# Attention and mixture of experts in one kernel: the transposes of K and pooled Q in half tiles, two groups a pair

## The chip, the cores and the metric

The kernel runs on one core of a Trainium2 chip. The metric is device time in microseconds (us) of one execution. Everything is float32 but a few small routing tables.

The engines are named as in the profile: PE (TensorE matmul; PEld is its weight load), DVE (VectorE), ACT (ScalarE), POOL (GpSimd) and SP (SyncE, which issues most DMA transfers). PE and the others meet in PSUM, the accumulator memory of eight banks; a bank holds 512 float32 in each of 128 partitions.

## The reference

q, k and v are 8 batches of 8 heads of 1152 rows of 64. Neighbouring rows of q are averaged, so 576 queries attend to 1152 keys. The 4608 attention rows of 512 then go through a mixture of 8 experts, each row through the one with the largest logit.

```python
q_pool = q.reshape(B, H, S // 2, 2, D).mean(axis=3)
scores = np.matmul(q_pool, k.transpose(0, 1, 3, 2)) / np.sqrt(D)
attn = np.exp(scores - scores.max(-1, keepdims=True))
x = heads_side_by_side(np.matmul(attn / (attn.sum(-1, keepdims=True) + 1e-9), v))
e, gate = argmax_and_its_probability(x @ w_gate)
out[row] = gate[row] * (np.maximum(x[row] @ w1[e[row]], 0) @ w2[e[row]])
```

## The kernel before

**Work.** Attention goes by batch (8) and by pair of heads (4 a batch, 32 in all). For a pair, `load_pair` loads K (`kn`), Q (`qn`) and V (`vn`), adds neighbouring rows of Q on POOL (`qp`; the first pair on DVE), orders K by row on ACT (`kp`), and turns both on PE, so that the 2 x 64 features of the two heads lie on the 128 partitions: `kT` (128 x 1152) and `qT` (128 x 576). PE turns a tile by a matmul with an identity (`nc.tensor.transpose`); the result lies in PSUM, and ACT copies it to `kT` or `qT`. This is done in groups, by the function `piece`.

`scores` then works a pair in two halves of 288 queries. For each of 9 chunks of 128 keys PE multiplies in four tiles of 64 x 64 at once into a buffer `st` of two banks, and DVE takes it out to `s` and finds a minimum on the way (line 525). There are two `st` buffers. After nine chunks PE spreads the minimum over the partitions (`spread`, line 543, which uses an `st` buffer too), DVE makes the bias, and ACT takes the exponent in three steps of three chunks (line 553). POOL adds the nine chunks to one in three steps, the folds (line 599), and PE adds up what they leave (line 608, into the bank `sums`). PE multiplies the exponents with V in nine chunks (`values`, line 624), again in four tiles.

There are two `fold` buffers and four buffers `s`. In the last three pairs PE does the sums without folds (line 594).

At the end of a batch the routing runs: row sums (line 644), logits (698), a turn (705), then on DVE the best expert, on PE the ranks (739 to 744), on DVE the places, and six scatters by POOL to lists in memory (`lists`, line 799). All of it uses the bank `sums`, which the next batch's first sum of folds needs. After the last batches POOL gathers the rows of the experts (`xr`, line 899), and the mixture of experts follows with two matmul stages (lines 1113 and 1141).

**Order.** A planner written in the kernel (`Flow`) sets the order on each engine. Each step has an engine, an assumed time and a key (a due time), and holds buffers. The planner plays the steps through and emits them in the order in which they came up, the lowest key first; a step whose buffer is not free is passed by. A step on PE has a tile shape (`COLS`, `QUADS`, or none for whole tiles); the planner stays with a shape as long as another with nearly the same key is ready. On the chip the engines run their lists in this order and wait for each other by semaphores.

PSUM before: two `st` buffers of two banks, one bank `m` (function `bank`) that holds a group of transposes, `pa` of two banks for the values, and `sums`.

## Time and profile before

| | |
|---|---|
| three timed runs, median (lowest to highest) | 1312.04 us (1309.75 to 1315.79) |
| the profiled execution, its own time | 1304.89 us |
| its span in the trace | 1303.3 us |
| busy over the span: PE, DVE, ACT, POOL | 94%, 59%, 49%, 66% |
| attention | until about 785 us, the mixture of experts behind it |

The span runs from the first to the last instruction of the trace. Busy time of PE counts a matmul until its modelled end, so matmuls side by side overlap in it. In the slices of the page each digit is a fortieth of the span, in tenths.

### The profile page before, as it was taken

What the parts mean: (1) busy time and instruction counts of PE and PEld (TensorE: products, weight loads), DVE (VectorE), ACT (ScalarE), POOL (GpSimd) and SP (SyncE); (2) the same over time, 40 slices, a digit from 0 to 9 for tenths busy, and PEclk for the clock granted to TensorE, in tenths of its full rate; (3) what the DMA queues carried; (4) which work ended last, traced back from release to release, by engine and by line L of the source; (5) the groups of instructions that cost most, each with busy time, mean ns of one, the idle gap of its engine ahead of it and who ended that gap; (6) DMA issues with size and microseconds to landing.
All of it is one profiled execution on the core that took longest, in us unless ns stands there. A gap on an engine that the chain in (4) does not pass through costs nothing. (4 is left out here: it accounts for less than half of the span.)

```text
span 1303.3 us, 32720 instructions
## 1 busy us (share of the span) xinstructions
PE 1222.0 (94%) x13677; PEld 844.5 (65%) x13677; DVE 771.5 (59%) x2080; ACT 637.5 (49%) x832; POOL 862.1 (66%) x539
## 2 busy tenths in 40 slices
PE   7999999999999999999999598898689889999995
PEld 3555555555555555555555157797578779899895
DVE  5777777767767768768776067663334435425440
ACT  4666666656666666666574046332223323424440
POOL 2999799798998998998992701577475755300110
PEclk8999999999999999999999699999798899999998
DMA  5523233323333333323324205652333434414330
GB/s 165 140 82 93 87 93 94 95 74 105 98 92 110 78 93 104 85 89 98 91 77 152 50 2 140 211 167 57 108 109 96 124 91 128 128 69 146 104 100 19
DMA packets 73517, 131.75 MB, mean 101 GB/s; under 512 B 9347, under 2 KB 32799, under 8 KB 73360
## 3 DMA queue, kind: packets, MB, share of 16 engines
q1 hardware_dynamic: 62528, 109.89, 28.8%
q0 software_dynamic: 9744, 19.64, 5.4%
q8 instruction: 110, 1.80, 0.7%
q14 instruction: 47, 0.39, 0.1%
q10 hardware_dynamic: 1088, 0.03, 0.1%
HBM read 108.75 MB, written 21.02 MB: 100 GB/s over the span
## 5 line engine op out<-in xcount | busy, mean ns | idle before, releaser
L525 DVE TENSOR_SCALAR_CACHE_REDUCE s<-st 128x576 f32<-128x576 f32 x576 | 424.5, 754 | 166.9 <-PE st L521 162.6
L553 ACT ACTIVATE s<-s,bias 128x1728 f32<-128x1728 f32 x192 | 325.3, 1733 | 172.5 <-DVE bias L549 168.2
L521 PE MATMUL st<-qT,kT 64*64 64x288 f32 x4608 | 374.8, 413 | 10.1 <-DVE bias L549 4.9
L624 PE MATMUL pa<-s,vn 64*64 64x288 f32 x4608 | 357.8, 405 | 3.6 <-issue 3.5
L521 PEld LDWEIGHTS st<-qT,kT 64*64 64x64 f32 x4608 | 160.5, 133 | 135.4 <-DVE s L525 30.0
L624 PEld LDWEIGHTS pa<-s,vn 64*64 64x64 f32 x4608 | 171.8, 133 | 102.9 <-issue 9.5
L599 POOL TENSOR_TENSOR fold<-s 128x1728 f32<-128x1728 f32 x58 | 224.3, 3875 | 14.3 <-ACT s L553 9.3
L599 POOL TENSOR_TENSOR fold<-fold,s 128x1728 f32<-128x1728 f32 x58 | 224.1, 3873 | 1.1
L1113 PE MATMUL ph<-xh,w1h 128*128 128x384 f32 (+6 forms) x512 | 162.9, 318 | 31.7 <-DVE hl L1121 22.0
L1113 PE MATMUL ph<-xl,w1h 128*128 128x384 f32 (+6 forms) x512 | 161.2, 315 | 0.7 <-DVE xl L1019 0.6
L1113 PE MATMUL ph<-xh,w1l 128*128 128x384 f32 (+6 forms) x512 | 160.8, 314 | 0.0
L1148 POOL DMA_INDIRECT out_dram<-y,rec x41 | 44.0, 1072 | 174.2 <-ACT y L1153 158.3
L899 POOL DMA_INDIRECT xr<-x_runs,ix x104 | 111.4, 1072 | 65.7 <-issue 26.8
L1121 DVE SCALAR_TENSOR_TENSOR hl<-ph,hh 128x384 fp32r<-128x384 f32 (+5 forms) x100 | 54.8, 550 | 148.3 <-ACT hh L1119 114.0
L1119 ACT ACTIVATE hh<-ph 128x384 fp32r<-128x384 f32 (+5 forms) x100 | 48.8, 488 | 187.4 <-PE ph L1113 139.6
L1141 PE MATMUL py<-w2h,hh 128*128 128x512 f32 x328 | 129.4, 394 | 4.0 <-issue 4.0
L1141 PE MATMUL py<-w2l,hh 128*128 128x512 f32 x328 | 129.0, 393 | 0.0
L1141 PE MATMUL py<-w2h,hl 128*128 128x512 f32 x328 | 128.9, 393 | 0.0
L1113 PEld LDWEIGHTS ph<-xh,w1h 128*128 128x128 f32 x512 | 100.8, 197 | 37.0 <-DVE hl L1121 25.0
L799 POOL DMA_INDIRECT lists<-re,di x48 | 44.7, 932 | 99.0 <-DVE di L759 65.7
L1113 PEld LDWEIGHTS ph<-xl,w1h 128*128 128x128 f32 x512 | 101.0, 197 | 1.9 <-DVE xl L1019 0.9
L1113 PEld LDWEIGHTS ph<-xh,w1l 128*128 128x128 f32 x512 | 100.9, 197 | 0.0
(176 smaller groups left out, 1372.6 us busy)
## 6 DMA issues: line engine op xcount, KB each, us to landing
raw<-in_moe_w_dram SPq DMA_DIRECT2D x80, 512.0 KB
kn<-in_k_dram SPq DMA_DIRECT2D x32, 576.0 KB
qn<-in_q_dram SPq DMA_DIRECT2D x32, 576.0 KB
vn<-in_v_dram SPq DMA_DIRECT2D x32, 576.0 KB
x_runs<-row SPq DMA_DIRECT2D x24, 396.0 KB
xr<-x_runs,ix POOLq DMA_INDIRECT x104
x_runs<-empty SPq DMA_DIRECT2D x4, 297.0 KB
lists<-re,di POOLq DMA_INDIRECT x48
```

The costliest lines, as they stand in the source:

```text
L521: nc.tensor.matmul(pt.t[to, h, :HQ], x.kT.t[up, c * P + i * D:c * P + (i + 1) * D], x.qT.t[up, cols], start=True, stop=True, tile_position ...
L525: nc.vector.tensor_scalar(s.t[:, c], pt.t[:, :, :HQ], -SCALE, None, op0=ALU.mult, op1=ALU.min, accum_out=mx.t[:, c:c + 1],)
L553: nc.scalar.activation(s.t[:, c0:c0 + n], s.t[:, c0:c0 + n], AF.Exp, bias=bias.t, scale=-1.0)
L599: add = lambda to, a, b: nc.gpsimd.tensor_tensor(to, a, b, ALU.add)
L624: nc.tensor.matmul(pa.t[cs, i, :HQ], x.vn.t[up, h, c, :], s.t[up, c, h], start=c == 0, stop=c == NC - 1, tile_position=(up.start, cs.start))
L799: ins = nc.gpsimd.indirect_dma_start(out=lists, out_offset=bass.IndirectOffsetOnAxis(ap=di.t[:, j:j + 1], axis=0), in_=re.t[:, j, :], in_o ...
L899: nc.gpsimd.indirect_dma_start(out=x.xr[i // NQD].t[:, i % NQD, :], out_offset=None, in_=xg, in_offset=bass.IndirectOffsetOnAxis(ap=x.ix.t ...
L1113: nc.tensor.matmul(view()[:, i, :], a[:, c, fp], b[:, c, :n], start=c == 0 and k == 0, stop=c == NDC - 1 and k == 2)
L1119: a = f.add("ACT", act(nb * n) - 44, lambda fs=fs, view=view: nc.scalar.activation(hidden(m)[0][:, fs, :n], view(), AF.Relu), at - 20, don ...
L1121: d = f.add("DVE", dve(nb * n), lambda fs=fs, view=view: nc.vector.scalar_tensor_tensor(hidden(m)[1][:, fs, :n], view(), 0.0, hidden(m)[0] ...
L1141: nc.tensor.matmul(py.t, a[:, c, hs], b[:, c % 2, :], start=c == 0 and k == 0, stop=c == NFC - 1 and k == 2)
L1148: nc.gpsimd.indirect_dma_start(out=out, out_offset=bass.IndirectOffsetOnAxis(ap=x.re.t[:up, r:r + 1], axis=0), in_=y.t[:up], in_offset=Non ...
```

## The change

K and the pooled Q are turned in half tiles: the 64 upper and the 64 lower rows of a tile are each turned by themselves (64 rows by 128 columns; of Q 48 and 64 rows, of which 48 are new), one into each of the two banks of an `st` buffer. For this Q is loaded in two transfers of 64 rows, the middle 32 rows twice. There are two groups a pair: one turns K's chunk 8 and all six of Q, the other K's chunks 0 to 7. The groups no longer use the bank `m`. ACT copies out K's chunk 8, Q, and K's other eight chunks in one instruction each, with the halves brought side by side. The steps have a tile shape of their own, `ROWS`, and other assumed times.

```diff
-COLS, QUADS = 1, 2
+COLS, QUADS, ROWS = 1, 2, 3
...
-        q0 = f.carry("SP", 480, lambda: load(qn.t, qb), key + K_LOAD, (), [qn], 2600)
+        q0 = f.carry("SP", 960, lambda: [load(qn.t[i * D:(i + 1) * D], qb[i * BL:i * BL + D]) for i in range(2)],
+                     key + K_LOAD, (), [qn], 2600)
...
-            pt = bank(o)
-            nk, n = len(ks) * P, len(ks) * P + len(qs) * QP
+            pt = hold_of("st", lambda h: o.ps_s.tile([P, 2, 512], F32, **h.own("st")))
+            nk = len(ks)
 
             def turn():
-                for i, c in enumerate(ks):
-                    nc.tensor.transpose(pt.t[:, i * P:(i + 1) * P], kp.t[:, c].rearrange("p h d -> p (h d)"), ident)
-                for i, j in enumerate(qs):
-                    nc.tensor.transpose(pt.t[:, nk + i * QP:nk + (i + 1) * QP], qp.t[:, j].rearrange("p h d -> p (h d)"),
-                                        ident[:QP, :QP])
-
-            s = f.add("PE", 0.9 * n, turn, key, after, [pt, *([kT, kp] if ks else []), *([qT, qp] if qs else [])])
+                for n, c in enumerate(ks):
+                    for i in range(2):
+                        up = slice(i * D, (i + 1) * D)
+                        nc.tensor.transpose(pt.t[:, i, n * D:(n + 1) * D], kp.t[up, c].rearrange("p h d -> p (h d)"),
+                                            ident[up, up], tile_position=(up.start, 0))
+                for n, j in enumerate(qs):
+                    for i, w in enumerate((QH, D)):
+                        up = slice(i * D, i * D + w)
+                        to = (nk + n) * D + (D - QH) * (1 - i)
+                        nc.tensor.transpose(pt.t[:, i, to:to + w], qp.t[up, j].rearrange("p h d -> p (h d)"),
+                                            ident[up, up], tile_position=(up.start, 0))
+
+            s = f.add("PE", 27 * 2 * (nk + len(qs)), turn, key, after, [pt, *([kT, kp] if ks else []), *([qT, qp] if qs else [])], ROWS)
...
-        piece(key, [], [0, 1, 2, 3, 4], done(q1))
-        piece(key + 2, [0, 1, 2, 3], [], done(k1))
-        piece(key + 4, [4, 5, 6, 7], [], done(k1))
-        piece(key + 6, [8], [5], done(k1, q1))
+        piece(key, [8], [0, 1, 2, 3, 4, 5], done(k1, q1))
+        piece(key + 4, [0, 1, 2, 3, 4, 5, 6, 7], [], done(k1))
```

Since a planner sets the order, the change moves more than the groups. On PE, in a steady batch, the order before has three of a pair's four groups here, between score chunks (`st<-qT,kT`), value chunks (`pa`) and a sum of folds (`sums<-fold`); a row is one or more matmuls of one kind, with its output, its operands and the size of one:

```order
L483 MATMUL m_5810<-ident,qp_5783 128x96 x5
L521 MATMUL st_5817<-qT_5352,kT_5397 64x288 x4
L521 MATMUL st_5825<-qT_5352,kT_5397 64x288 x4
L608 MATMUL sums_5403<-fold_5674,ones_73 32x288 x4
L481 MATMUL m_5842<-ident,kp_5614 128x128 x4
L624 MATMUL pa_5848<-s_5504,vn_5056 64x288 x8
L521 MATMUL st_5858<-qT_5352,kT_5397 64x288 x4
L481 MATMUL m_5863<-ident,kp_5614 128x128
L483 MATMUL m_5863<-ident,qp_5783 128x96
```

In the new order both groups of a pair stand in one piece; ahead of these rows stand a sum of folds, two half tiles of K's chunk 8 and ten of Q:

```order
L493 MATMUL st_4533<-ident,qp_4211 128x48
L493 MATMUL st_4533<-ident,qp_4211 128x64
L487 MATMUL st_4549<-ident,kp_4213 128x64 x16
L634 MATMUL pa_4570<-s_4283,vn_3726 64x288 x4
L553 MATMUL st_4576<-ident,top 64x64 x4
L634 MATMUL pa_4570<-s_4283,vn_3726 64x288 x8
L531 MATMUL st_4593<-qT_4188,kT_4186 64x288 x4
```

So the groups moved from between the scores to behind a sum of folds, and the two `st` buffers that they fill are those that the spread (`st_4576`) and the next score chunk need.

On POOL, the order before has the six scatters of a batch (`lists`) spread over several halves, with the folds of two halves interleaved:

```order
L465 TENSOR_TENSOR qp_4091<-qn_3985 96x2x6x64
L599 TENSOR_TENSOR fold_3983<-fold_3983 128x576
L799 DMA lists<-re_4167,di_4192 42240x2 x2
L599 TENSOR_TENSOR fold_4250<-s_3835 128x1728
L799 DMA lists<-re_4167,di_4192 42240x2
L599 TENSOR_TENSOR fold_4250<-fold_4250,s_3835 128x1728
L599 TENSOR_TENSOR fold_4354<-s_3944 128x1728
L599 TENSOR_TENSOR fold_4250<-fold_4250 128x576
```

The new order has four of the six scatters in a row and the other two within the next half's fold:

```order
L466 TENSOR_TENSOR qp_4211<-qn_3926 128x2x6x64
L609 TENSOR_TENSOR fold_4132<-fold_4132,s_3915 128x1728
L609 TENSOR_TENSOR fold_4132<-fold_4132 128x576
L809 DMA lists<-re_4302,di_4318 42240x2 x4
L609 TENSOR_TENSOR fold_4397<-s_4048 128x1728
L809 DMA lists<-re_4302,di_4318 42240x2
L609 TENSOR_TENSOR fold_4397<-fold_4397,s_4048 128x1728
L809 DMA lists<-re_4302,di_4318 42240x2
L609 TENSOR_TENSOR fold_4397<-fold_4397 128x576
```

The scatters moved together, ahead of the fold of the next batch's third half, and the halves' folds no longer interleave there.

## Rows read from the trace of the kernel before

**Rows 1.** The page: busy us (share of the span) of each engine, and the busy tenths of PE and POOL in 40 slices.

```profile
PE 1222.0 (94%) x13677; PEld 844.5 (65%) x13677; DVE 771.5 (59%) x2080; ACT 637.5 (49%) x832; POOL 862.1 (66%) x539
...
PE   7999999999999999999999598898689889999995
...
POOL 2999799798998998998992701577475755300110
```

**Rows 2.** Windows of the attention part, cut at the routing logits of each batch: the stretch, its length, then busy us (and instructions) of PE, PEld, DVE, ACT and POOL, the granted TensorE clock, the DMA share and GB/s. Left out are two of the four steady batches, which read the same.

```profile
30.00:129.00 99.00, 99.00 (x1533) 58.09 (x1533) 71.83 (x208) 65.78 (x78) 98.08 (x35) 1.00 0.38 103
129.00:224.00 95.00, 91.77 (x1391) 52.54 (x1392) 67.53 (x201) 58.42 (x74) 83.58 (x34) 1.00 0.30 90
224.00:313.70 89.70, 89.46 (x1359) 51.06 (x1357) 64.73 (x198) 57.48 (x60) 81.05 (x34) 1.00 0.32 88
313.70:404.30 90.60, 90.42 (x1374) 51.68 (x1372) 66.50 (x200) 58.16 (x72) 85.05 (x35) 1.00 0.34 94
...
585.70:676.30 90.60, 90.39 (x1373) 51.65 (x1372) 66.44 (x200) 58.12 (x72) 85.01 (x35) 1.00 0.35 93
```

**Rows 3.** The waits of POOL in one steady batch (404.3 to 495 us): who waited for whom, us in total, times, longest.

```profile
POOL lists L799 <- DVE top L546: 3.7, 1, 3.7
POOL fold L599 <- PE st L521: 0.8, 1, 0.8
POOL lists L799 <- issue: 0.6, 3, 0.3
POOL lists L799 <- PE st L521: 0.2, 1, 0.2
```

**Rows 4.** The timeline of POOL at the first two scatters of that batch: start, length, engine, line, output<-input, and in brackets the idle time before it with what ended it.

```profile
416.79 0.92 POOL L799 DMA_INDIRECT lists<-re,di  x1 [3.65 <-DVE top L546]
418.01 0.92 POOL L799 DMA_INDIRECT lists<-re,di  x1 [0.30 <-issue]
```

**Rows 5.** The timeline of PE at several places of steady batches, in order of time; consecutive matmuls of one kind are merged (x8 is one chunk in four tiles and two passes), and the length reaches to the modelled end of the last. From 479.91 to 484.28 values and scores alternate, a chunk each.

```profile
303.07 0.66 PE L521 MATMUL st<-qT,kT 64*64 64x288 f32 x8
303.67 0.66 PE L481 MATMUL m<-ident,kp 128*128 128x128 f32 x4
304.26 1.20 PE L521 MATMUL st<-qT,kT 64*64 64x288 f32 x16
305.28 1.64 PE L624 MATMUL pa<-s,vn 64*64 64x288 f32 x24
...
310.24 0.29 PE L543 MATMUL st<-ident,top 64*64 64x64 f32 x8
...
313.17 0.63 PE L483 MATMUL m<-ident,qp 96*128 96x96 f32 x5
313.74 1.18 PE L698 MATMUL sums<-xT,wg 128*32 128x288 f32 x16
...
413.72 0.22 PE L739 MATMUL sums<-cnt,ones_bf 96*96 96x48 bf16 x1
...
479.91 0.66 PE L624 MATMUL pa<-s,vn 64*64 64x288 f32 x8
...
484.28 0.66 PE L521 MATMUL st<-qT,kT 64*64 64x288 f32 x8
```

**Rows 6.** Groups of instructions over the whole span, in the order of their cost: line, engine, operation, output<-input, sizes, count, then busy us and the mean ns of one, then the idle time before them and what ended it.

```profile
L525 DVE TENSOR_SCALAR_CACHE_REDUCE s<-st 128x576 f32<-128x576 f32 x576 | 424.5, 754 | 166.9 <-PE st L521 162.6 <-POOL fold L599 1.5
...
L553 ACT ACTIVATE s<-s,bias 128x1728 f32<-128x1728 f32 x192 | 325.3, 1733 | 172.5 <-DVE bias L549 168.2 <-DVE xr L1056 3.3
L599 POOL TENSOR_TENSOR fold<-s 128x1728 f32<-128x1728 f32 x58 | 224.3, 3875 | 14.3 <-ACT s L553 9.3 <-PE st L521 4.8
L599 POOL TENSOR_TENSOR fold<-fold,s 128x1728 f32<-128x1728 f32 x58 | 224.1, 3873 | 1.1
...
L599 POOL TENSOR_TENSOR fold<-fold 128x576 f32<-128x576 f32 x58 | 81.5, 1413 | 0.7
L465 POOL TENSOR_TENSOR qp<-qn 96x768 f32<-96x768 f32 x31 | 56.4, 1820 | 20.5 <-DMA qn<-in_q_dram 15.8 <-PE m L483 4.6
...
L489 ACT COPY kT<-m 128x512 f32<-128x512 f32 (+1 forms) x96 | 45.6, 475 | 33.9 <-PE m L481 20.3 <-PE m L483 13.4 <-issue 0.2
L799 POOL DMA_INDIRECT lists<-re,di x48 | 44.7, 932 | 99.0 <-DVE di L759 65.7 <-DVE top L546 24.5 <-issue 7.2
...
L493 ACT COPY qT<-m 128x480 f32<-128x480 f32 x64 | 25.4, 397 | 20.6 <-PE m L483 20.4
...
L543 PE MATMUL st<-ident,top 64*64 64x64 f32 x512 | 20.5, 225 | 2.7 <-issue 1.6 <-DVE top L546 1.1
```

**Rows 7.** The page's DMA issues: the load of Q, with the size of one transfer.

```profile
qn<-in_q_dram SPq DMA_DIRECT2D x32, 576.0 KB
```

**Rows 8.** The timeline of PE in the opening, the second and third group of transposes of the first pair.

```profile
9.73 1.12 PE L481 MATMUL m<-ident,kp 128*128 128x128 f32 x4 [0.68 <-ACT kT L489]
11.52 1.06 PE L483 MATMUL m<-ident,qp 96*128 96x96 f32 x5 [0.68 <-ACT kT L489]
```

**Rows 9.** The timelines of PE and of POOL behind the last folds, from the first to the last of a row of gathers on POOL (in between PE's rows read like the second).

```profile
715.98 5.77 PE L594 MATMUL sums<-s,ones 128*32 128x288 f32 x58
743.69 1.12 PE L624 MATMUL pa<-s,vn 64*64 64x288 f32 x2 [1.46 <-issue]
745.36 1.00 POOL L899 DMA_INDIRECT xr<-x_runs,ix  x1 [0.30 <-issue]
```

20 lines of the change are left out of this document (12 added, 8 removed).

## The prediction

> **What bounds the kernel now.** I read the busy shares first, then one batch of the steady part engine by engine, then the rows of the places that the change touches.
>
> The page puts PE at 94% and POOL at 66% of the span, and in the slices POOL is full only in the first 21 of 40, which is the attention part [rows 1]. The windows cut that part at the routing matmul of each batch. From 313.7 to 676.3 us four batches take 90.65 us each, and in them PE is busy 90.4 us (99.7%), POOL 85.1, DVE 66.5, ACT 58.2 [rows 2]. So PE sets the pace there and POOL follows 5.5 us behind per batch. The reader should see how near the second bound is: POOL has 5.5 us of idle time in a batch, and a gain on PE arrives only as far as that shrinks. In the first 99 us after the opening POOL is busy 98.1, so there nothing is left to win.
>
> POOL's idle time in one steady batch is one wait of 3.65 us and small pieces [rows 3]: the first of the six list scatters waits for the routing result of the batch before. 90.65 - 85.1 - 3.65 leaves 1.9 us of gaps that belong to the scatters and to the order.
>
> **What PE does in a batch.** A chunk of scores or values (eight matmul records, four tiles in two passes) starts 0.485 us after the one before: from 479.91 to 484.28 nine of them [rows 5]. A batch has 144 of these, 69.8 us. Eight sums of folds take 0.485 each, 3.9; the routing logits two such, 1.0; eight spreads about 0.11 each, 0.9; the small routing matmuls about 1.2 (0.5 for the row sums, 0.33 for three turns, 0.4 for the ranks). The transposes: four of K last 0.66 with 0.27 for the last one's own length, so 0.13 apart; five of Q 0.63 with 0.25, so 0.096 apart [rows 5, 6]. 36 of K and 24 of Q are 4.7 + 2.3 = 7.0. That makes 83.8 us; the other 6.85 of 90.65 are the changes between tile shapes. In PE's order of before a batch has 44 of them, counted through one period of the repeating order, so 0.156 us each. A single one agrees: from the score chunk at 303.07 to the K transposes at 303.67 are 0.60, 0.115 above a chunk, and the chunks behind them need 1.02 for two instead of 0.97 [rows 5].
>
> **The change part by part.**
>
> *Transposes.* A pair has 15 slots of two transposes, 64 moved columns each, in the two row halves at once. The nearest row is the spread: eight records of 64 columns, in two rounds of four tiles, last 0.29 with a mean of 0.225 for one, so a round follows the other in about 0.06 [rows 5, 6]. 60 slots a batch at 0.06 are 3.6 us instead of 7.0. From below the slot is not under 0.06, since the round of 64 columns is that long; from above every half could take what a whole tile takes now, 120 x 0.13 = 15.6. I take 0.06, because four tiles with two row halves already load and multiply side by side in that row. The Trainium skill (TensorE: Matmul & The Clock Gate, LDWEIGHTS) speaks against the change: a weight load's time goes by its columns, about columns/1.2 ns, and not by its rows, so half tiles of 128 columns would load no faster, an estimate of 107 ns for each. By it the slots would cost 6.4 us a batch if both halves load together, and nothing would be won on the transposes themselves. The Q transposes, each with a load of 128 columns, stand 96 ns apart, so the trace does not bear out the 107.
>
> *Groups.* Two groups a pair instead of four, and in the order of after both stand back to back, three of four pairs right behind a sum of folds, which has a change of shape anyway. Counted through one period of the new order a batch has 25 changes: 25 x 0.156 = 3.9 instead of 6.85. PE's work becomes 83.8 - 7.0 + 3.6 + 3.9 = 84.3 us a batch, 6.35 less than now.
>
> *Evictions.* ACT copies kT and qT of a pair in 3 instructions instead of 5. Now they cost (45.6 + 25.4)/32 = 2.2 us a pair [rows 6]. A mean kT copy of 384 elements takes 0.475 and the exponent over 1728 takes 1.733, so 100 elements cost 0.094 and an instruction 0.115 by itself: 1728 elements in three are 1.97, a gain of 0.25. ACT has 32 us free a batch: nothing on the path.
>
> *Score buffers.* The groups now hold the two score buffers, which DVE empties at 0.75 a chunk [rows 6], until ACT has copied them. In the new order one to three value chunks stand behind the groups, 0.5 to 1.5 us; the first group's two copies, 128 and 576 elements, take about 0.9. So the next score finds a buffer if ACT starts at once. If ACT is in an exponent, up to 1.73 us are added. Lower end 0, upper end 1.73 four times a batch, 6.9 us. I take 0 to 0.3 each, since in ACT's new order the copies stand behind exponents that by their spread are done by then.
>
> *Loads.* Q comes in two transfers of 64 rows, 768 KB instead of 576, one more issue on SP per pair [rows 7]. 192 KB x 32 are 6.3 MB; at 94 GB/s the DMA share is 0.34 [rows 2], and POOL's waits in a steady batch name no load [rows 3]. Behind the second issue on SP wait only the load of V and the stores of rows, which nobody waits for that early. Nothing. The pooling on POOL is 768 elements a row as before, on 128 rows instead of 96: 1.82 us [rows 6].
>
> **Where the time goes next: POOL.** Its work in a batch is eight folds of 3.875 + 3.873 + 1.413 = 9.16, four poolings of 1.82 and six scatters of 0.92 [rows 6]: 73.3 + 7.3 + 5.5 = 86.1 by the sum, 85.1 by the busy time (starts overlap ends by some 0.08). I walked the new order through one batch with these durations. The ranks on PE are followed by the places on DVE, and the scatters that wait for them: from 413.72 to 416.79 in one batch, 3.1 us [rows 4, 5], of which I give the places 2.5. In the new order four scatters come in a row, from start to start 1.22 [rows 4], 4.9 together, then a fold with two scatters between its parts, 9.2 + 2.2. PE meanwhile has 31 chunks, two sums and two spreads until it needs that fold: 17.3 us after the ranks, POOL is ready after 19.1. So PE waits about 1.8 us there, in a run of eight scores without values, and from there POOL works back to back until the next scatters: 4.9 + 11.4 + 7 x 9.16 + 4 x 1.82 = 87.7, and 0.5 + 0.3 us for two exponents that come just in time: 88.5 us. The other loop, from the last fold of a batch through row sums, logits, ranks and places to the scatters, is 17.5 + 2.5 + 0.5 us, and POOL has two folds and a pooling, 20.2 us, for it: about even, so the 3.65 us wait of now goes.
>
> **Sum.** Four steady batches from 90.65 to 88.5: 8.6 us. The batch from 224 to 313.7 (89.7): 1.2. The one from 129 to 224 holds 11.4 us of POOL's idle time [rows 2]; I take half of what lies over 88.5, 3.2. The first batch: 0.9 of idle POOL; and in the opening the second and third group wait 0.68 each for ACT to clear the single bank [rows 8], of which two buffers save perhaps 0.7. The last three pairs have no folds, but from 716 to 746 PE gets through little beside the row gathers on POOL [rows 9], which stays; about 1 us. Together 16 us. The profiled execution took 1304.89 us (span 1303.3), so 1289; the median of the three timed runs is 1312.04, 7.15 higher, and with the same distance I say 1296.
>
> **The rivals.**
>
> *PE's whole gain arrives (POOL's idle time goes).* For it: POOL has 5.5 us a batch to give. Against: the walk leaves it no earlier start. At 87.0 a batch (85.1 + 1.9) the four give 14.6, the two before 2.7 + 8, the ends 3.5: 29 us, so 1283. Chance 0.14.
>
> *It doesn't do what it says: nothing arrives.* POOL's wait moves instead of going, because logits now stand behind more values and the ranks come 17.5 us after the fold instead of about 14. If 2 us of wait stay, the period is 90.5: 1311, within 0.5%. Chance 0.17.
>
> *The two halves load or multiply one after the other.* 120 x 0.06 = 7.2 a batch puts PE at 87.9, just under POOL's 88.5, with both full about 89.5: 8 us, 1304. At 0.13 each PE is at 96.3: 5.65 x 6.5 batches, 37 us more, 1349. For it: no row shows 64x128 tiles. Against: rows of 64x64 tiles overlap. Chance 0.08 for the first, 0.03 for the second.
>
> *The score buffers stop PE (the other side).* If one exponent stands ahead of each pair of groups' copies, PE loses 1.73 us four times a batch, at places where POOL then starves too. It decides from 2.15/4 = 0.54 us a time on; at 1.73 it is 4.8 us a batch, 31 in all: 1343. The Trainium skill (TensorEngine Tiling (Array Packing), PSUM Bottleneck) says the same in general: tiles speed up TensorE, not the emptying of PSUM. In this trace ACT is busy 58.2 of 90.65 us [rows 2], so a third of its time is free for the copies. Chance 0.1.
>
> **How the numbers follow.** The forecast has 0.48. Faster by over 0.5% (6.6 us, about what a measurement of this kernel tells from no change) are the forecast but for its slow end (0.46), the full gain (0.14) and most of the mild serial case (0.06): 0.66. Same: 0.17 + 0.02 + 0.02, 0.21. Slower: 0.03 + 0.1, 0.13. The range goes from just below the full gain, 1280, to the case in which nothing arrives, 1312; it leaves out the two slow cases and little more. The forecast's own range is 1288 to 1304.
>
> **What would show it.** Right: the 30 transposes of a pair standing two at a time, some 0.06 from slot to slot; steady batches of 88 to 89 us; POOL over 96% busy in them and PE at about 95%, with PE idle ahead of a sum of folds; scores hardly waiting for ACT. Wrong: halves 0.06 or more apart each; waits of scores for kT or qT copies of a microsecond; the 3.65 us wait ahead of the scatters still there; or PE still full at 90 us a batch.

## The result and the profile after

The changed kernel is slower: 1325.76 us (median of four runs, 1322.64 to 1328.01) against 1310.89 for the kernel before (four runs), a ratio of 1.011 with a 95% interval of 1.008 to 1.0145. The forecast was 1296. The profiled execution took 1328.01 us, span 1326.5; it is the slowest of the four, so the two profiles lie 23 us apart where the medians lie 15 apart.

The page of the changed kernel, busy us of each engine [rows 1]: the work went down on PE, and its share went down more.

```profile
PE 1209.7 (91%) x14157; PEld 830.4 (63%) x14157; DVE 770.0 (58%) x2080; ACT 627.6 (47%) x768; POOL 866.0 (65%) x539
```

Windows of the changed kernel, cut at the routing product of each batch, columns as in [rows 2]:

```profile
125.90:216.50 90.60, 87.11 (x1436) 49.79 (x1432) 65.81 (x200) 56.97 (x64) 85.77 (x35) 1.00 0.36 103
...
403.20:496.80 93.60, 88.67 (x1436) 49.81 (x1432) 66.52 (x200) 56.87 (x64) 85.33 (x35) 0.98 0.37 99
...
684.50:815.10 130.60, 102.45 (x1287) 53.12 (x1286) 64.59 (x203) 46.65 (x48) 39.99 (x34) 0.84 0.20 60
```

The second batch takes 90.6 us where it took 95.3; the steady ones take 93.8 in the mean where they took 90.65, with PE and POOL both idle more (4.9 and 8.3 us in the second row); and the last interval, before the routing product of the eighth batch, takes 130.6 where it took 118.2 (676.3 to 794.5). Behind it, in the expert part, little moved (511.4 us against 508.8). So the loss stands in two places, and the gain of the first two batches (7.7 us at the second product) is used up by the fifth.

The transposes are what they were meant to be. PE's timeline of the changed kernel at one pair's two groups:

```profile
436.84 0.27 PE L487 MATMUL st<-ident,kp 64*128 64x64 f32 x2
436.95 0.54 PE L493 MATMUL st<-ident,qp 48*128 48x48 f32 x12
437.31 0.67 PE L487 MATMUL st<-ident,kp 64*128 64x64 f32 x16
437.92 0.71 PE L634 MATMUL pa<-s,vn 64*64 64x288 f32 x8
```

Thirty transposes in 1.08 us, 0.072 for a slot of two. What is new stands at the four scatters. POOL's timeline of the changed kernel in the same batch:

```profile
415.48 0.92 POOL L809 DMA_INDIRECT lists<-re,di  x1 [1.83 <-DVE bias L559]
416.71 0.92 POOL L809 DMA_INDIRECT lists<-re,di  x1 [0.30 <-issue]
417.93 0.92 POOL L809 DMA_INDIRECT lists<-re,di  x1 [0.30 <-issue]
419.15 0.92 POOL L809 DMA_INDIRECT lists<-re,di  x1 [0.30 <-issue]
420.08 3.86 POOL L609 TENSOR_TENSOR fold<-s 128x1728 f32<-128x1728 f32 x1
```

VectorE's timeline of the changed kernel beside it:

```profile
417.06 0.45 DVE L639 TENSOR_TENSOR xT<-xT,pa 128x288 f32<-128x288 f32 x1
421.24 0.76 DVE L535 TENSOR_SCALAR_CACHE_REDUCE s<-st 128x576 f32<-128x576 f32 x1 [3.73 <-remote]
```

And PE's timeline there:

```profile
417.21 1.20 PE L531 MATMUL st<-qT,kT 64*64 64x288 f32 x16
418.23 1.21 PE L634 MATMUL pa<-s,vn 64*64 64x288 f32 x16
422.06 1.24 PE L531 MATMUL st<-qT,kT 64*64 64x288 f32 x8 [2.62 <-DVE s L535]
```

"Remote" means that the profile names no instruction that ended the wait. The semaphore records in the trace say more: what VectorE waits for here is PE's semaphore. By their modelled ends the two score chunks are done at 417.93 and 418.41, but PE's signals for them are counted at 421.21 and 421.31, 3.3 and 2.9 us later, where the median over the whole trace is 0.04. So the signal is late, and VectorE starts with it. Whether the matmuls themselves ended late or only their signals, the trace can't tell, since their ends are modelled.

VectorE itself is not held by a row as such. In the kernel before, POOL issues six scatters in a row from 688.78 to 695.81, and VectorE works among them once a first signal of PE (2.4 us late) has come. VectorE's timeline of the kernel before:

```profile
693.02 0.15 DVE L828 COPY fn<-m 1x8 f32<-1x8 f32 x1 [1.88 <-remote]
693.10 0.43 DVE L629 TENSOR_TENSOR xT<-xT,pa 128x288 f32<-128x288 f32 x1
...
695.68 0.15 DVE L836 TENSOR_TENSOR feq<-feq,rev 1x8 f32<-1x8 f32 x1
```

Where the text below says that a row stops VectorE, it means this: VectorE waits for a signal of PE that comes late. In the changed kernel the wait ends 1.2 us after the last scatter of the row, it comes in every steady batch (3.68 to 3.75 us), and PE, with both score buffers full, stands still for 2.62 us of it. In this execution the clock follows; windows of 2 us of the changed kernel, the granted clock is the third column from the right:

```profile
420.00:422.00 2.00, 0.00 (x0) 0.00 (x0) 0.76 (x3) 0.48 (x1) 1.99 (x2) 0.86 0.13 46
422.00:424.00 2.00, 1.94 (x16) 0.99 (x20) 1.32 (x4) 0.00 (x0) 1.94 (x1) 0.50 0.02 6
...
426.00:428.00 2.00, 2.00 (x40) 1.20 (x36) 1.52 (x5) 0.00 (x0) 2.00 (x1) 1.00 0.09 8
```

After the idle stretch PE runs at 0.50, the 1.2 GHz level, and starts 16 matmuls in 2 us where it starts 40 two windows later.

In the last interval the same thing is larger. VectorE's longest wait there, of the changed kernel:

```profile
DVE s L535 <- remote: 37.1, 3, 23.7
```

and of the kernel before, a row that I had not read:

```profile
DVE bias L549 <- remote: 30.6, 1, 30.6
```

In the changed kernel these are one wait behind a row of six scatters (5.0 us) and two beside a row of 24 gathers; in the kernel before it is one beside the 24 gathers [rows 9]. The semaphore is again PE's: the spread's last matmul ends at 729.99 by its record, and its signal is counted at 749.37, 19.4 us later. PE itself gets on slowly there, with gaps that the profile puts down to nothing. One value chunk, which lasts 0.66 us in a steady batch [rows 5], reaches from 735.98 to 744.81 in PE's timeline of the kernel before:

```profile
735.98 0.74 PE L624 MATMUL pa<-s,vn 64*64 64x288 f32 x1
737.36 1.45 PE L624 MATMUL pa<-s,vn 64*64 64x288 f32 x2 [0.64 <-issue]
739.50 0.72 PE L624 MATMUL pa<-s,vn 64*64 64x288 f32 x1 [0.69 <-issue]
```

### The profile page after: what moved, and what is told of

Its sections match the earlier page's. It is cut to its first block, busy times and chain, and to the rows that moved or that the text cites. A ratio compares the mean times of both kernels' runs of the same rounds, so it can differ in the third digit from the quotient of the medians.

```text
span 1326.5 us, 33648 instructions
## 1 busy us (share of the span) xinstructions
PE 1209.7 (91%) x14157; PEld 830.4 (63%) x14157; DVE 770.0 (58%) x2080; ACT 627.6 (47%) x768; POOL 866.0 (65%) x539
## 5 line engine op out<-in xcount | busy, mean ns | idle before, releaser
L535 DVE TENSOR_SCALAR_CACHE_REDUCE s<-st 128x576 f32<-128x576 f32 x576 | 417.5, 753 | 216.2 <-PE st L531 157.9
L563 ACT ACTIVATE s<-s,bias 128x1728 f32<-128x1728 f32 x192 | 320.3, 1729 | 230.9 <-DVE bias L559 230.7
L531 PE MATMUL st<-qT,kT 64*64 64x288 f32 x4608 | 368.6, 418 | 44.3 <-DVE s L535 29.7
L609 POOL TENSOR_TENSOR fold<-s 128x1728 f32<-128x1728 f32 x58 | 224.4, 3870 | 35.6 <-ACT s L563 35.1
```

The costliest lines, as they stand in the source:

```text
L531: nc.tensor.matmul(pt.t[to, h, :HQ], x.kT.t[up, c * P + i * D:c * P + (i + 1) * D], x.qT.t[up, cols], start=True, stop=True, tile_position ...
L535: nc.vector.tensor_scalar(s.t[:, c], pt.t[:, :, :HQ], -SCALE, None, op0=ALU.mult, op1=ALU.min, accum_out=mx.t[:, c:c + 1],)
L563: nc.scalar.activation(s.t[:, c0:c0 + n], s.t[:, c0:c0 + n], AF.Exp, bias=bias.t, scale=-1.0)
L609: add = lambda to, a, b: nc.gpsimd.tensor_tensor(to, a, b, ALU.add)
```

## The experiments

Theories: **A**, rows of scatters or gathers on POOL stop VectorE, and the change made such rows; **B**, the groups in the score buffers stop PE (the rival on record); **C**, the order on PE costs the time whatever POOL does. The table gives for each run the routing product of the second, seventh and eighth batch (us), the steady period (mean of the last three to four steady batches), the interval before the eighth, and the ratio to the kernel before on the same chip with its interval.

| kernel | 2nd | 7th | 8th | period | last interval | ratio |
|---|---|---|---|---|---|---|
| before | 224.2 | 676.3 | 794.5 | 90.65 | 118.2 | 1 |
| after | 216.5 | 684.5 | 815.1 | 93.8 | 130.6 | 1.011 (1.008 to 1.0145) |
| e2_row | 226.0 | 690.7 | 809.1 | 93.3 | 118.4 | 1.012 (1.008 to 1.016) |
| e1_spaced | 218.0 | 670.2 | 799.1 | 91.0 | 128.9 | 1.0035 (0.9997 to 1.007) |
| e4_whole | 215.8 | 667.3 | 791.9 | 90.3 | 124.6 | 0.996 (0.993 to 0.998) |
| e6_half | 214.2 | 660.2 | 786.7 | 89.2 | 126.5 | 0.993 (0.990 to 0.996) |
| e11_three | 215.9 | 668.7 | 795.8 | 90.6 | 127.1 | 1.007 (1.004 to 1.011) |
| e5_four | 229.0 | 723.1 | 852.1 | 98.7 | 129.0 | 1.049 (1.045 to 1.053) |
| e7_gap | 216.6 | 678.2 | 805.8 | 91.9 | 127.6 | 1.009 (1.006 to 1.013) |
| e8_whole_gap | 215.9 | 669.4 | 794.3 | 90.7 | 124.9 | 0.998 (0.995 to 1.001) |
| e12_early3 | 213.5 | 659.7 | 746.9 | 89.2 | 87.2 | 0.972 (0.968 to 0.975) |
| e13_early1 | 213.1 | 659.2 | 750.8 | 89.2 | 91.6 | 0.967 (0.962 to 0.971) |
| r_after | 215.8 | 677.0 | 807.2 | 92.2 | 130.2 | 1.016 (1.0125 to 1.020) |
| r_half | 213.0 | 659.1 | 785.2 | 89.2 | 126.1 | 0.991 (0.987 to 0.995) |
| r_before1 | 224.4 | 676.4 | 763.6 | 90.6 | 87.2 | 0.973 (0.968 to 0.979) |
| r_early1 | 212.6 | 658.7 | 750.5 | 89.2 | 91.8 | 0.966 (0.962 to 0.969) |

### A row put into the kernel before, and taken out of the changed one

e2_row, in the loop over the six scatters of the kernel before:

```diff
+            if b is not None and b < B - 2 and j < 4:
+                if j == 0:
+                    outs.append(f.carry("POOL", 4 * 1230, lambda: [enlist(i) for i in range(4)], at, done(p, *hold), [di, re], 40))
+                continue
```

> The kernel before with one edit: the first four scatters of a batch are one step of POOL, so that they stand in a row as they do in the changed kernel; transposes, groups and buffers are those of before. Theory A: VectorE stands still for 3.7 us at that place in each steady batch, the period of 90.65 us grows by 2.5 to 4 us, and the time goes to 1322 to 1332 us. Theories B and C: nothing of the transposes or of the order of scores and values changes (but for a few steps), so 1308 to 1314 us.

VectorE's timeline of e2_row at the row (scatters from 517.40 to 521.99):

```profile
519.67 0.44 DVE L629 TENSOR_TENSOR xT<-xT,pa 128x288 f32<-128x288 f32 x1
523.19 0.76 DVE L525 TENSOR_SCALAR_CACHE_REDUCE s<-st 128x576 f32<-128x576 f32 x1 [3.07 <-remote]
```

The stop is there in each steady batch (3.05 to 3.11 us), the period grows by 2.6 us and the median was 1318.30 against 1301.04 on that chip. My range of 1322 to 1332 was drawn from a kernel before of 1312; the 17 us of growth lie within its 10 to 20. A is right, and B and C are not needed for it: nothing of the transposes was touched.

e1_spaced, the same loop in the changed kernel:

```diff
-            outs.append(f.carry("POOL", 1230, lambda j=j: enlist(j), at + ..., done(p, *hold), [di, re], 40))
+            outs.append(f.carry("POOL", 1230, lambda j=j: enlist(j), at + ...,
+                                done(p, *hold, *(outs[-1:] if j and b is not None and b < B - 2 else ())), [di, re], 40))
```

> The changed kernel with one edit: from the second scatter of a batch on, each waits in the plan for the transfer of the one before it (not in the last two batches), so that POOL does a fold or a sum between two scatters and never four in a row. Theory A (four scatters in a row on POOL stop VectorE for 3.7 us once a batch, and TensorE, ScalarE and POOL behind it): no wait of VectorE for 3.7 us is left in the steady batches, their period falls from 93.7 us to between 88.5 and 90.7, and over five batches 15 to 26 us go: 1300 to 1311 us. Theory B (the two groups of transposes hold the score buffers, and that is what slows VectorE and TensorE): the transposes are where they were, the period stays at 93 to 94 us and the time at 1322 to 1328. Theory C (the order of scores and values on TensorE costs the time whatever the scatters do): the period stays within 1 us of 93.7 although the stall is gone. On the interval before the last routing product (130.5 us against 118.2) A says nothing, since the six scatters of that batch stay in a row.

POOL's timeline of e1_spaced, where a fold now stands between two scatters:

```profile
410.23 0.92 POOL L809 DMA_INDIRECT lists<-re,di  x1 [2.13 <-DVE di L769]
412.20 3.86 POOL L609 TENSOR_TENSOR fold<-s 128x1728 f32<-128x1728 f32 x1 [1.05 <-PE sums L618]
416.21 0.92 POOL L809 DMA_INDIRECT lists<-re,di  x1
```

No remote wait is left before the last interval. The batches take 93.8 and 88.2 us in turn, since the order repeats every two, 91.0 in the mean. So the steady loss is mostly gone, with a period 0.3 us over what A allowed. That 1307.25 lies where A said is luck: the kernel before is 10 us faster on this chip than on the changed kernel's, and by the ratios (1.0035 against 1.011, and 1.016 for r_after below) 10 to 17 us are gone where A said 15 to 26. The last interval, as expected, kept 128.9.

### What the half tiles and the two groups are worth

e4_whole keeps two groups in score buffers and turns whole tiles, each into one bank:

```diff
...
-                    for i in range(2):
-                        up = slice(i * D, (i + 1) * D)
-                        nc.tensor.transpose(pt.t[:, i, n * D:(n + 1) * D], kp.t[up, c]..., ident[up, up], tile_position=(up.start, 0))
+                    i, to = (n // (len(ks) // 2), n % (len(ks) // 2) * P) if len(ks) > 1 else (0, 0)
+                    nc.tensor.transpose(pt.t[:, i, to:to + P], kp.t[:, c]..., ident)
```

> Two groups a pair in score buffers, as in the changed kernel, but of whole tiles (128 and 96 rows) as before, each tile to one bank. POOL's order has at most two scatters in a row. Theory A: no stop of 3.7 us, so faster than the changed kernel though the transposes take 3 to 3.5 us a batch longer on TensorE: 1303 to 1315 us. Theory B: the score buffers are held as in the changed kernel and longer, 1325 to 1340 us. Theory C: the order on TensorE is nearly that of the changed kernel, so 1320 to 1330 us.

It took 1295.92 us: far under what B and C said, and under A's range too, on a chip where the kernel before takes 1301.04.

e6_half is the changed kernel with the planner told another length of the groups:

```diff
-            s = f.add("PE", 27 * 2 * (nk + len(qs)), turn, key, after, [pt, ...], ROWS)
+            s = f.add("PE", 0.9 * (len(ks) * P + len(qs) * QP), turn, key, after, [pt, ...])
```

> The changed kernel with one edit: the planner is told of its transposes what it was told in e4_whole (0.9 ns a column, no tile shape), so that the order of every engine is the order of e4_whole, and half tiles against whole tiles is all that differs between the two. POOL has at most two scatters in a row in the steady batches. Theory A (rows of four or more scatters and gathers stop VectorE; the half tiles do what they were meant to): steady period between 87.5 and 89.5 us against the 90.3 of e4_whole, total 6 to 20 us below e4_whole on the same chip, so a ratio to the kernel before of 0.982 to 0.991. Rival H (half tiles cost as much in changes of the tile shape as they save in slots): the period stays within 0.3 us of 90.3 and the ratio within 0.003 of 0.996. Rival G (TensorE no longer sets the pace once the transposes stand in two groups, VectorE's taking of scores does): the transposes are 2 us a batch shorter in the rows, the waits for VectorE grow by as much, and the period does not move.

PE's timeline of e4_whole from a pair's first transpose to the next chunk:

```profile
423.25 0.33 PE L482 MATMUL st<-ident,kp 128*128 128x128 f32 x1
...
424.89 0.72 PE L625 MATMUL pa<-s,vn 64*64 64x288 f32 x8
```

and of e6_half at the same place of the same order:

```profile
419.13 0.28 PE L487 MATMUL st<-ident,kp 64*128 64x64 f32 x2
...
420.21 0.71 PE L634 MATMUL pa<-s,vn 64*64 64x288 f32 x8
```

1.64 us against 1.08, so 2.2 us a batch less; the period fell by 1.1. Where the other half went no row shows. PE's weight loads do wait for VectorE, in one batch of e6_half:

```profile
PEld st L531 <- DVE s L535: 8.6, 17, 1.3
```

of e4_whole:

```profile
PEld st L522 <- DVE s L526: 8.2, 16, 1.3
```

and of the kernel before:

```profile
PEld st L521 <- DVE s L525: 3.2, 11, 0.5
```

So this wait came with the two groups, not with the half tiles. A holds in part: half tiles win 1.1 us a batch, and e6_half takes 1292.23 against 1303.13 us for the kernel before, but by the ratios that is 4 us below e4_whole where A said 6 to 20. Rival G, as put, does not hold, since the period moved and the wait hardly grew. And the one edit between the changed kernel and e6_half is a number in the plan: with 378 and 432 ns for the two groups the planner puts four scatters in a row, with 634 and 922 ns two. That alone turns 1.011 into 0.993, each against the kernel before on its chip. (The tile shape that the edit also drops from the plan moves nothing: with the new length, the order on POOL and PE is the same with it and without it.)

e5_four turns half tiles in the four groups of before, each in a score buffer:

```diff
...
-        piece(key, [8], [0, 1, 2, 3, 4, 5], done(k1, q1))
-        piece(key + 4, [0, 1, 2, 3, 4, 5, 6, 7], [], done(k1))
+        piece(key, [], [0, 1, 2, 3, 4], done(q1))
+        piece(key + 2, [0, 1, 2, 3], [], done(k1))
+        piece(key + 4, [4, 5, 6, 7], [], done(k1))
+        piece(key + 6, [8], [5], done(k1, q1))
```

> Half tiles as in the changed kernel, but in the four groups of before, each with a score buffer of its own, so that the score buffers are taken four times a pair and not twice. POOL's order has two scatters in a row in most batches, three in some. Theory A: most of the stop of VectorE is gone, 1300 to 1315 us. Theory B: twice as many groups stand between scores and their buffers, so the time is above that of the changed kernel: 1330 to 1345 us. Theory C names no number, since the order is a third one; by it the period would be neither that of before nor that of the changed kernel, and no single wait would explain the difference.

1363.01 us, beyond what B said, with no remote wait before the last interval and only two waits of 2.1 us behind rows of three scatters. PE's timeline of e5_four, behind a pair's first two groups:

```profile
527.98 0.77 PE L487 MATMUL st<-ident,kp 64*128 64x64 f32 x10 [0.67 <-ACT qT L504]
...
530.58 1.76 PE L534 MATMUL st<-qT,kT 64*64 64x288 f32 x16 [1.77 <-ACT kT L499]
```

and ScalarE's:

```profile
528.31 1.75 ACT L566 ACTIVATE s<-s,bias 128x1728 f32<-128x1728 f32 x1
529.95 0.75 ACT L499 COPY kT<-st 128x512 f32<-128x512 f32 x2
```

Here B is real: the copy that would free the score buffer stands behind an exponent. With two groups a pair the same wait is 0.9 us a batch at most in e6_half. What the rest of the eight us a batch is was not separated.

e11_three brings two numbers of the plan nearer to the rows, and three scatters come in a row:

```diff
-            s = f.add("PE", 27 * 2 * (nk + len(qs)), turn, ...
+            s = f.add("PE", 62 * (nk + len(qs)), turn, ...
-            m = f.add("PE", 460, product, ...      (scores; the values likewise)
+            m = f.add("PE", 486, product, ...
```

> The changed kernel with two numbers of the plan nearer to the rows: 62 ns instead of 54 ns a pair of half tiles, 486 instead of 460 ns a product. The order that comes out has three scatters in a row in a steady batch instead of four (then one, one, one). Theory A with the stop growing from the length of the row: a stop of 0 to 2.5 us, a period of 89.5 to 92.5 us, 1295 to 1312 us. Theory C (the order on TensorE, with runs of up to five scores in place of eight): a period under that of the changed kernel by less than 1 us and no link to the stop.

VectorE's timeline of e11_three at its row of three (scatters from 409.34 to 412.71):

```profile
413.65 0.76 DVE L535 TENSOR_SCALAR_CACHE_REDUCE s<-st 128x576 f32<-128x576 f32 x1 [1.81 <-PE st L531]
```

It is the same wait, though the profile names PE here and not "remote": it ends 0.95 us after the last scatter, with a signal that comes 1.4 us behind the chunk's modelled end. VectorE's waits go with the row's length: two scatters in a row, none of this size (signals 0.9 to 1.1 us late); three, 1.8; four, 3.1 to 3.7; six, 5.0 in the changed kernel; 24 gathers, 30.6. The length sets only how long a signal can be late, as the 1.9 us beside the six scatters of the kernel before show: there a signal came within the row.

### What ends the stops

e7_gap (the changed kernel) and e8_whole_gap (e4_whole) put a short write on POOL behind every scatter and gather:

```diff
                 in_=re.t[:, j, :], in_offset=None, bounds_check=NE * LIST - 1, oob_is_err=False,
             )
+            nc.gpsimd.memset(gap, 0.0)
... (the same behind each of the 148 gathers)
```

> The changed kernel with a small write of zeros on POOL (128x64) behind every scatter and every early gather; nothing else is changed, and the order of all other work is the same. If what stops VectorE is that POOL issues indirect transfers without any other instruction between them (theory A1), the stops of 3.7 us (rows of four), 5 us (row of six) and 24 + 8 us (24 gathers) are gone, the period falls to 89.5 to 91.5 us, the stretch of the gathers is no longer idle on TensorE, and the total falls by 20 to 45 us against the changed kernel, to 1280 to 1305 us. If it is that the transfers themselves are under way (theory A2), a write of a fraction of a us changes nothing: the stops stay within 0.5 us of what they were, plus the time of the writes on POOL, and the total is 1320 to 1335 us.

> e4_whole with the same write of zeros on POOL behind every scatter and early gather. There the steady batches have no stop to lose, so this shows the last stretch alone: by A1 the 24 gathers no longer stop VectorE (31 us in all there) and the total falls by 10 to 28 us below e4_whole, a ratio of 0.975 to 0.988 to the kernel before; by A2 it stays within 3 us of e4_whole, a ratio of 0.994 to 0.999.

VectorE's waits of e7_gap from 494 to 805 us:

```profile
DVE s L536 <- remote: 43.5, 6, 12.7
```

The writes take 0.17 us each, and most stops stay (2.9 to 3.7 us in rows of four, one of 0.7; 31 us beside the gathers, but in three pieces). e7_gap's 1313.67 us lie between the two ranges, so neither A1 nor A2 holds as I had put them: the gap is mostly too short. e8_whole_gap, 1297.57 us, kept its last interval, as A2 said.

e9_copy asks whether the addition ahead of each stop is the cause:

```diff
-            xT.t[:, hp, to], xT.t[:, hp, to], pa.t[:, 1, :HQ], ALU.add), key + 20, done(p, a), [pa, xT])
+            xT.t[:, hp, to], pa.t[:, 1, :HQ]), key + 20, done(p, a), [pa, xT])      (tensor_copy)
```

> The changed kernel with one edit: the addition on VectorE that puts the second half of the keys to the attention output (it reads xT and the sums in PSUM) is a copy of the sums alone, so the output leaves the first half of the keys out, and the routing is that of other numbers; order, rows of scatters and everything else stay. In each steady batch the stop of VectorE began right behind this addition. Theory A3 (VectorE is caught when, in a row of scatters, it has an instruction that reads two operands or SBUF): with the copy, which reads PSUM alone, the stop of 3.7 us in the steady batches is gone or comes later behind another such instruction and is under 2 us, and the period falls to 90 to 92 us. Theory A2 (the row itself stops VectorE whatever it runs): the stop stays between 3 and 3.8 us and the period between 93 and 94.5 us. The total is not to be compared, since the routing differs.

VectorE's timeline of e9_copy:

```profile
418.10 0.45 DVE L639 COPY xT<-pa 128x288 f32<-128x288 f32 x1
422.15 0.76 DVE L535 TENSOR_SCALAR_CACHE_REDUCE s<-st 128x576 f32<-128x576 f32 x1 [3.60 <-remote]
```

The stop stays with a copy that reads PSUM alone, so A3 falls. The period, 92.2 us, lies between the two ranges; it is that of the changed kernel's own order in r_after (below), where the clock reads 1.00 as it does here, and A2's range came from an execution that reads 0.98. The Trainium skill (SBUF — State Buffer, SBUF: two separate sides) has a port pair that VectorE and GpSimd lock against each other, for one instruction at a time, VectorE with two SBUF inputs or in a two-port mode. These rows don't fit that: what stands still reads PSUM, and it stands through two whole scatters of 0.92 us and beyond. It waits for PE's signal, which comes at 422.12, 3.2 us late.

e10_tail and e12_early3 put 1.6 us of writes, e13_early1 0.53, between the early gathers and between the six scatters of the last batch but one (e10_tail: of the last two), in e6_half's order:

```diff
... (behind each scatter likewise, if b == B - 2)
+            for _ in range(3 if early else 0):      (e13_early1: 1)
+                nc.gpsimd.memset(gap, 0.0)          (gap: 128x512)
...
-        x.rows = done(*(f.carry("POOL", 1310, lambda i=i: gather(i), ...
+        x.rows = done(*(f.carry("POOL", 2900 if early else 1310, lambda i=i: gather(i), ...      (1840)
```

> e6_half with three writes of zeros (128x512, about 1.5 us together) on POOL behind each of the 24 early gathers and each scatter of the last two batches; the steady batches stay as they are. If VectorE is let in whenever POOL does something else for over a us between two indirect transfers (A1 with a longer gap), the stops of 4.6 and of 13 + 20 us shrink to less than 2 us each, TensorE works through the stretch of the gathers, which itself grows from 31 to about 65 us, and the last interval falls from 126.5 to 105 to 118 us: ratio to the kernel before 0.977 to 0.987. If the writes do not let it in (A2), the stop grows with the stretch to 60 us and the total to 1310 to 1325 us, a ratio of 1.005 to 1.017.

In e10_tail my edit stood behind all 148 gathers (24 are early; 124 follow, not the 80 that the next text names), and the plan did not know of the writes. The stops went, but the expert part now waited for gathers; VectorE's longest waits there:

```profile
DVE xr L1072 <- DMA xr<-x_runs,ix: 170.1, 18, 17.1
```

1474.66 us. It says that writes of this length end the stops, and nothing of what that is worth.

> e6_half with three writes of zeros (128x512) on POOL behind each of the 24 early gathers and each scatter of the last batch but one, and with the plan told of their time. In e10_tail they stood behind the 80 later gathers too, which made POOL the bound of the expert part, and the plan did not know of them. Theory A1 with a long gap: no stop of VectorE over 2 us in the last interval, TensorE works through the stretch of the gathers (some 70 us), the last interval is 105 to 118 us in place of 126.5, the expert part is as long as in e6_half, total 8 to 22 us below e6_half, a ratio to the kernel before of 0.976 to 0.987. Rival: the work of the expert part that needs the gathers stands in VectorE's order ahead of the last scores and values, and later gathers make VectorE wait for them in place of the stop: the last interval stays at 124 to 130 us and the ratio at 0.990 to 0.997.

> As e12_early3 with one write of zeros (0.53 us) in place of three, so that the stretch of the gathers is about 45 us and not 70. If half a us between two gathers lets VectorE in, as 1.5 us did, the last interval is 108 to 120 us and the ratio 0.978 to 0.990; if it is too short, as the 0.17 us of e7_gap was, stops of over 5 us are left and the ratio is 0.989 to 1.000.

Both beat both kernels: 1263.74 and 1258.88 us against 1301.79, more than I expected, since the last interval fell to 87.2 and 91.6. Half a microsecond is enough where 0.17 was not.

### The same in the kernel before, and all on one chip

e14_before1 is the edit of e13_early1 in the kernel before, e15_after1 the same in the changed kernel with a write behind each steady scatter too:

```diff
+            for _ in range(1 if b == B - 2 else 0):                         (e14_before1)
+            for _ in range(1 if b is not None and b < B - 1 else 0):        (e15_after1)
+                nc.gpsimd.memset(gap, 0.0)
... (behind each early gather, and in the plan, as above)
```

> The kernel before with one write of zeros (128x512, 0.53 us) on POOL behind each of the 24 early gathers and each scatter of the last batch but one, and the plan told of it. Theory A: the stop of 30.6 us goes here too, the last interval falls from 118.2 to 90 to 100 us, the steady batches stay at 90.65, total 18 to 28 us below the kernel before, a ratio of 0.978 to 0.986; e13_early1 is then 10 to 18 us faster than this, which is the change itself. Rival: the kernel before has less work left at the gathers (104 products and values behind them in place of 130) and gains little: a ratio of 0.988 to 0.996.

> The changed kernel in its own order, with the same write of zeros behind every scatter up to the last batch but one and behind each early gather. Theory A (the stops are the loss): no stop of 3 us or more is left, the period falls from 93.7 to between 89 and 91.3 us, the last interval from 130.5 to 90 to 100 us, and the total is 1260 to 1275 us, a ratio of 0.967 to 0.979. Theory C (the order costs the steady batches their time): the period stays above 92 us without stops, the last interval falls as in A, and the total is 1275 to 1290 us, a ratio of 0.979 to 0.991.

These two fell on a chip where the kernel before takes 1246.65 us (13 runs). e14_before1 took 1246.61 there, a ratio of 0.999 (0.998 to 1.001), and e15_after1 1266.86, a ratio of 1.016: in the kernel before the writes gain nothing on that chip. No signal of PE comes over 0.1 us late in either trace, and in e14_before1 that holds beside rows without writes too, of two scatters in the steady batches and of up to 22 gathers in the expert part. So that chip has no late signals. e15_after1 still has a period of 93.0, which speaks for C; but its writes fill POOL, as a window of it shows,

```profile
589.20:682.20 93.00, 88.34 (x1436) 50.59 (x1432) 66.36 (x200) 57.01 (x64) 88.28 (x41) 0.98 0.37 100
```

and PE's weight loads wait 4.1 us a batch there for folds, against 2.1 in e6_half. So A fails by its number, and C is not shown either; the changed kernel without writes was not run on that chip. The four runs that followed are the changed kernel, e6_half, e14_before1 and e13_early1 unchanged, on one chip where the kernel before took 1298.88:

> The changed kernel once more, on one chip with the next three. If the chip has the stops (the kernel before at about 1302 us): a ratio to the kernel before of 1.008 to 1.016, stops of 3.7 us a batch. If it has none (the kernel before at about 1247 us): by theory A no loss is left, period 88.5 to 91 us and a ratio of 0.985 to 1.000; by theory C the order alone costs it, period 92 to 93.5 us and a ratio of 1.008 to 1.018.

> e6_half once more. With stops: a ratio of 0.990 to 0.996. Without: the steady batches still gain 1.1 to 1.4 us each, and the last interval, which was 8.3 us longer than that of the kernel before, has no stop to lengthen it, so a ratio of 0.985 to 0.993.

> e14_before1 once more. With stops: by theory A the last interval falls from 118 to 85 to 95 us and the ratio is 0.974 to 0.986; by its rival (little work left behind the gathers) 0.988 to 0.996. Without stops: the ratio stays at 0.998 to 1.001, as it was.

> e13_early1 once more. With stops: a ratio of 0.962 to 0.971, and against r_before1 8 to 16 us less by theory A. Without stops: within 3 us of r_half, a ratio of 0.985 to 0.995.

That chip has the stops, and the four came as expected or just beyond it (r_after 1.016, r_before1 0.973): r_before1's last interval went down from 118 to 87 us. Where the gain comes from is seen in the stretch of the gathers, which is longer with the writes; a window of the kernel before,

```profile
719.00:746.00 27.00, 15.46 (x55) 4.18 (x51) 0.00 (x0) 0.00 (x0) 20.61 (x22) 0.69 0.24 53
```

and of r_early1:

```profile
693.60:734.90 41.30, 40.26 (x640) 22.09 (x632) 28.52 (x80) 20.70 (x16) 37.54 (x47) 1.00 0.33 90
```

VectorE does nothing at all in 27 us of the one and works 28.5 of 41.3 in the other; PE goes from 55 matmuls in 27 us at a clock of 0.69 to 640 in 41.3 us at full. r_early1 is 8.3 us faster than r_before1 (1254.15 against 1262.42): about that is what half tiles in two groups, in e6_half's order, bring where the early rows stop nothing, and the writes are worth some 35 us in either kernel.

## Why the prediction was wrong

**The walk through POOL's new order** is the step that failed. I saw the four scatters in a row and gave them 4.9 us of POOL, back to back. That is about what they take (4.6 us, 415.48 to 420.08), and POOL's wait ahead of them did shrink, from 3.65 to 1.83 us. What the step had no term for is what the row does to the other engines: PE's signals come up to 3.3 us late, VectorE stands still for 3.7 us, PE for 2.62 of it, and in the profiled execution 1.2 GHz follows. By e2_row a row of four costs a batch 2.6 us. Instead of 88.5 us the period came to 92.2 to 93.8.

**The last three pairs**, "about 1 us", is the larger term: +12 us. I read rightly that PE gets through little beside the gathers [rows 9] and took it as something that stays. It is a wait of VectorE of 30.6 us for a signal of PE, and its cost depends on how much work for PE and VectorE is left behind it. In the changed kernel 61 us of the last interval lie behind the gathers, in the kernel before 48. With the stops gone the interval is 87 us in the kernel before and 92 in e6_half's order, so the stops cost 31 us in the one and 34 in the other (126.1 to 91.8). The other 5 us of the 8 between these two are likely work that the new order leaves for later. What makes the changed kernel's interval 4 us longer still was not separated.

**PE's work.** The slots came out 20% over what I took (0.072 for 0.06), and of what they save only a part reached the period. Two groups in place of four, 2.95 us a batch by the sum for their changes of shape, brought 0.35 (e4_whole, 90.3), and half tiles, 3.4 by the sum, another 1.1 (e6_half, 89.2). That 89.2 is near the forecast 88.5 is in part luck, since the reason given was POOL back to back: POOL is busy 85.3 of 89.2, and PE's weight loads wait 8.6 us for VectorE's taking of scores, 5.4 more than before.

**The score buffers**: 0 to 0.3 us was right for ScalarE's copies with two groups; the rival's mechanism, an exponent ahead of the copy, showed only with four groups (e5_four). **Loads and evictions** cost nothing that the steady waits show, as said. **The first two batches** gained 3.0 and 4.7 us, more than the 1.6 and 3.2 of the sum; the third, forecast to gain 1.2, already lost 3.2.

So the forecast that half tiles in two groups help held in another order (e6_half, r_early1), and the change as planned lost by a row of transfers that its plan happened to make and by a longer last interval. How the changed kernel's steady loss splits exactly is open: taking e2_row's price off r_after's 92.2 leaves 89.6, e1_spaced says 91.0, and e15_after1 could not tell.

## What to carry to other kernels

When a scheduler is told new durations, compare where its order puts runs of the same instruction, and look at the other engines beside any such run that the trace already has; a "remote" wait of 30 us in the trace of before held the answer. For such a wait, look up which semaphore ended it: here it is PE's, and the engine that stands still is not the one that is late. A transfer on POOL is priced by what a row of them holds up elsewhere, not by its own 0.92 us: where a trace shows such waits, put half a microsecond of other work between two of them. And a stop late in a stage costs what is left behind it, so a change that shifts work past it can lose there what it saves elsewhere.

## What the runs showed of the hardware

- Beside indirect transfers that POOL issues one behind the other, PE's semaphore signals come late: by 0.9 to 1.1 us in rows of two, 1.4 in rows of three, 3.3 in rows of four, 6.1 in a row of six of the changed kernel and 19.4 beside 24 gathers, against a median of 0.04. VectorE, which waits for them, mostly goes on about 1 us (behind gathers 3 us) after the last transfer, and works through a row where it needs nothing of PE. In the long rows PE's own matmuls slow down too. What holds them up no run shows.
- A write of 0.17 us on POOL between two transfers ends the stops now and then; with one of 0.53 us a single stop of 3.0 us was left in r_before1, and none in e13_early1 and r_early1.
- The expert part has such waits too: in the kernel before, beside 19 gathers (905 to 930 us), a signal of PE comes 10.3 us late and VectorE idles 8.0 us. No run put writes there in a way that could gain: e10_tail's were too many.
- Not every chip does it: on one the kernel before took 1247 us instead of about 1300, the writes changed nothing in it there, and no signal of PE in the two traces taken there (e14_before1, e15_after1) is over 0.1 us late. The unchanged kernel has no trace on that chip.
- After a wait of 2.6 us PE ran at 0.50 of its clock for a few us in the first profiled execution of the changed kernel; in r_after, with the same wait of 2.6 us, the steady windows read 1.00, and the period was 1.6 us shorter.
- Two transposes of 64 rows by 128 columns, in the two row halves and to two PSUM banks, follow each other in 0.072 us a slot: fifteen tiles in 1.08 us against 1.64 for whole ones.
